# Attention and token/channel mixer on one core: a new fixed order for every engine's queue

## The chip, the cores and the metric

The kernel runs on 1 core of one Trainium2 chip. The metric is the device time of one execution in microseconds (us), as the median of the runs shown. The engines that the text speaks of are TensorE (PE, with its weight loads as PEld), VectorE (DVE), ScalarE (ACT), GpSimd (POOL) and SyncE (SP), which issues all DMAs of this kernel.

## What is computed

Attention with a decay, for 8 batches x 8 heads of 576 tokens x 64, and behind it a mixer over tokens and one over channels. All inputs are float32.

```python
def _attn_ref(q, k, v, f):                       # q, k, v: (8, 8, 576, 64), f: (8, 8, 576)
    scores = scale * np.matmul(q, k.transpose(0, 1, 3, 2))
    cum = np.cumsum(np.log(np.clip(f, 0.0001, 1.0)), axis=-1)
    decay = cum[:, :, :, None] - cum[:, :, None, :]
    scores = np.where(causal, -1000000000.0, scores + decay)
    attn = np.exp(scores - np.max(scores, axis=-1, keepdims=True))
    attn = attn / (np.sum(attn, axis=-1, keepdims=True) + 1e-09)
    return np.matmul(attn, v)

def _moe_ref(x, w_tok1, w_tok2, w_ch1, w_ch2):   # x: (8, 576, 512), the heads side by side
    xt = x.transpose(0, 2, 1)
    u = x + (np.maximum(xt @ w_tok1, 0.0) @ w_tok2).transpose(0, 2, 1)
    return u + np.maximum(u @ w_ch1, 0.0) @ w_ch2
```

The weights come as float64 and are decoded on the chip: w_tok1 is 576 x 256, w_tok2 256 x 576, w_ch1 512 x 1536, w_ch2 1536 x 512.

## The kernel before, in words

**Stages.** Head by head (n = 0 to 63) the kernel computes the scores of five query tiles (64 rows and four times 128), cut to the columns that the causal mask leaves. One PE operation makes tile 4 (`s4`), one tiles 0 and 3 (`s3`), one tiles 2 and 1 (`s2`), all at L1083. DVE takes the negated row maximum (L1085), ACT the exponential with its sum (L1088), DVE the reciprocal (L1092, L1095), POOL scales (L1110), PE transposes (L1130, L1163), ACT and DVE copy the transposes into SBUF, and PE multiplies with v (L1187, L1224). The first four heads multiply in float32 from q and k as loaded (tile `xt`, lines L1061 and L1189 to L1197 of the trace); the others split q, k and v into a high and a low part (`hl`, `vv`). After four heads half of a batch's token mixer follows (`mixer`), after eight the rest and two of the twelve column blocks of the channel mixer. Behind the last head come 512 tokens of the channel mixer in the plain way, and then four steps of 1024 tokens with a seven-product scheme (`big`), lines L1544 to L1546 and L1606 to L1608 of the trace.

**The weights** are decoded between the heads: a DMA of the raw float64 words (L817), an ACT step (L829), two DVE steps (L833, L837), and for the token mixer's weights a high part on ACT (L729) and a low part on POOL (L735).

**The order.** `build` makes a list of 5697 operations with their engine, an estimated duration, what they read and write, and the rotating buffers that they use. Each has a number from the table `PR` (kind k0 to k127, one number for each operation of the kind), which replaces the planner's due time. `Plan.run` replays the list: at each moment an engine that is free takes, among the operations that are ready and whose buffers are free, the one with the lowest number. An operation that isn't ready is passed over. The operations are then emitted in the order of the replay, under a manual schedule, so on the chip each engine runs its queue in that order and waits at each instruction for what it needs. In the table before, the numbers of each engine are all different, and they are the places in which the trace shows that engine's instructions.

**Buffers.** `run` gives each operation its buffers, the first that is free. Heads 0 and 2 share one buffer for q and k (`qf`), heads 1 and 3 the other. Scores of tiles 0 to 3, transposes and mixer products rotate through four banks of PSUM (`one`); the scores of tile 4 have one pair of banks (`sc`).

**Idle products.** `idle` (L803) is a product of 16 x 128 whose result nobody reads. `PRM["FILL"]` = 112 of them go ahead of the first real PE operation; later ones go where the replay has PE idle for more than 0.5 us (0.7 us behind 50 us), a gap's length less a margin, divided by 65 or 85 ns, up to the channel mixer.

**The first places of SP's queue**, with the size of each load, are those that the change moves most:

| place | before | KB | after | KB |
|---|---|---|---|---|
| 0, 1 | f, two halves | 72 each | f, two halves | 72 each |
| 2 | w_tok1 | 128 | w_tok1 | 128 |
| 3 | raw q, k of heads 4, 5 (half) | 288 | w_tok1 | 256 |
| 4 | w_tok1 | 128 | w_tok1 | 128 |
| 5 | w_tok1 | 256 | **q, k of head 0** | 288 |
| 6 | w_tok1 | 256 | raw q, k of heads 4, 5 (half) | 288 |
| 7 | w_tok1 | 256 | raw q, k of heads 4, 5 (half) | 288 |
| 8 | raw q, k of heads 4, 5 (half) | 288 | w_tok1 | 256 |
| 9 | **q, k of head 0** | 288 | w_tok1 | 256 |
| 10 | **q, k of head 1** | 288 | **q, k of head 1** | 288 |
| 11 | v of heads 0, 1 | 320 | w_tok1 | 256 |
| 12 | decay rows of head 4 | 4.5 | w_tok2 | 288 |
| 13 | w_tok1 | 256 | **q, k of head 2** | 288 |
| 14, 15 | w_tok2; decay rows of head 5 | 288; 4.5 | decay rows of head 2 | 2.25 each |
| 16 | gather for head 4 | 288 | v of heads 0, 1 | 320 |
| 17 to 19 | decay rows; w_tok2; gather | 4.5; 288; 288 | w_tok2; gather; q, k of head 3 | 288 each |
| 20 | **q, k of head 2** | 288 | w_tok2 | 288 |
| 21, 22 | decay rows of head 2 | 2.25 each | decay rows of head 3; gather | 2.25; 288 |
| 23 | v of heads 2, 3 | 320 | w_tok2 | 288 |

v of heads 2 and 3 stands at place 37 after, behind weight loads at places 34 and 35.

Of the kernel before, what the change touches and what calls it, by code (L numbers as in the profile page):

```python
# [15 lines left out]
P = 128  # L16

PRM = dict(
    P1=(-60, -56, -52, -48, -44), P2=(-12, -8, -4, 0, 4), E1="DDDDD", E2="DDDDD", TK=4, TU=5, PE=0, HS=(-4, -3, 19, 21), XS=(0.5, 0.6, 12, 20), HE="DDDD", XE="DDDD", WE="D", CE="D", RE="P", FILL=112, ED=False, EP=3, DB=0, DLAST=1, F1=2, FQ=4, FV=4, LAG=3.88, n_raw=1, n_vr=2, n_hl=1, n_k1=2, n_k2=2, n_vv=2,
# [5 lines left out]
    k1=(0, 1,),  # L25
# [3 lines left out]
    k5=(2,),  # L29
    k6=(3,),  # L30
    k7=(4,),
    k8=(6,),
    k9=(1, 0,),
    k10=(4, 7, 2, 6,),
    k11=(1, 3, 5, 8, 9, 10,),
    k12=(2, 4, 5, 6, 7, 13, 14, 18, 24, 31, 34, 37, 38, 39, 40, 43, 55, 57, 56, 58, 75, 73, 72, 74, 91, 108, 121, 123, 122, 124, 128, 126, 132, 127, 145, 160, 180, 178, 183, 184, 179, 181, 182, 185, 209, 215, 239, 236, 240, 232, 238, 235, 241, 233, 286, 287, 299, 296, 300, 298, 309, 311, 310, 312, 329, 338,),
    k13=(3, 5, 10, 11, 14, 17, 21, 29, 40, 43, 53, 55, 61, 72, 86, 85, 111, 178, 179, 206, 223, 254, 269, 299, 303, 347, 359, 390, 396, 470, 476, 499, 509, 543, 564,),
    k14=(8, 7, 13, 16, 21, 25, 33, 42, 52, 53, 63, 67, 81, 82, 99, 129, 142, 216, 217, 244, 250, 306, 305, 348, 346, 410, 411, 477, 478, 527, 529, 564, 566, 615, 649,),
    k15=(10, 9, 15, 19, 24, 27, 45, 44, 54, 56, 65, 71, 83, 104, 106, 143, 185, 218, 224, 246, 277, 309, 307, 364, 380, 412, 414, 511, 512, 530, 549, 582, 601, 618, 653,),
    k17=(8, 7, 12, 15, 19, 22, 39, 38, 47, 48, 58, 63, 79, 98, 104,),  # L40
    k18=(12, 11, 13, 14, 15, 16, 28, 27, 34, 35, 36, 43, 49, 59, 64,),
    k19=(11, 23, 47, 59, 67, 77, 89, 104, 114, 142, 156, 174, 195, 211, 229, 256, 271, 285, 302, 328, 343, 360, 373, 394, 410, 421, 438, 455, 465, 478, 491, 502,),
    k20=(11, 5,),
    k21=(6, 4,),
    k22=(9, 10, 20, 26,),
# [12 lines left out]
    k35=(44, 64, 82, 96,),  # L58
    k36=(22, 21, 28, 29,),
    k37=(62, 64, 68, 118, 123, 124, 184, 186, 190, 249, 251, 254, 328, 329, 332, 380, 383, 388, 466, 469, 476, 507, 513, 517, 582, 584, 590, 637, 638, 642, 704, 711, 722, 768, 771, 774, 845, 854, 857, 894, 905, 907, 968, 983, 986, 1010, 1011, 1013,),  # L60
    k38=(101, 103, 152, 157, 214, 216, 278, 279, 353, 354, 403, 405, 484, 488, 523, 531, 594, 595, 644, 645, 703, 708, 760, 763, 830, 837, 871, 883, 942, 955, 973, 974,),
    k39=(109, 112, 172, 175, 240, 242, 311, 312, 393, 394, 445, 447, 538, 542, 581, 588, 663, 664, 712, 713, 783, 788, 846, 848, 918, 925, 964, 976, 1041, 1053, 1069, 1070,),
    k40=(109, 158, 222, 281, 358, 412, 493, 534, 601, 646, 719, 766, 839, 885, 957, 976,),
    k41=(116, 176, 248, 314, 397, 455, 546, 592, 670, 717, 800, 851, 927, 978, 1054, 1072,),
# [32 lines left out]
    k74=(509, 519,),  # L97
    k75=(106, 161, 218, 288, 339,),
    k76=(195, 239, 285, 328, 377, 427, 486, 507, 558, 598,),
    k77=(243, 276, 344, 367, 446, 476, 547, 599, 650, 667,),  # L100
    k78=(144, 159, 201, 210, 258, 270, 308, 336, 361, 370,),
    k79=(130, 189, 244, 313, 362,),
    k80=(376, 380, 381, 382, 529, 530, 531, 544, 545, 547,),
# [25 lines left out]
    k106=(526,),  # L129
# [1966 lines left out]
```

## Time and profile before

| | us |
|---|---|
| median of 3 runs (lowest, highest) | 1028.75 (1024.60, 1030.69) |
| span of the profiled execution, from its first to its last instruction | 1021.2 |
| PE busy in it | 1007.6 |
| DVE, ACT, POOL busy | 813.4, 694.8, 421.4 |
| mean granted TensorE clock, as a share of the full one | 0.999 |

The page gives of the profiled execution the span, not its time with what lies around it. A busy time is the sum of an engine's instructions with overlaps counted once; PE's includes the idle products. Rows of the timeline merge instructions of one line: start, length, engine, line, operation, shapes, count, and in brackets how long the engine stood idle ahead of the first and what ended that.

### The profile page before, as it was taken

What the parts mean: (1) busy time and instruction counts of PE and PEld (TensorE: products, weight loads), DVE (VectorE), ACT (ScalarE), POOL (GpSimd) and SP (SyncE); (2) the same over time, 40 slices, a digit from 0 to 9 for tenths busy, and PEclk for the clock granted to TensorE, in tenths of its full rate; (3) what the DMA queues carried; (4) which work ended last, traced back from release to release, by engine and by line L of the source; (5) the groups of instructions that cost most, each with busy time, mean ns of one, the idle gap of its engine ahead of it and who ended that gap; (6) DMA issues with size and microseconds to landing.
All of it is one profiled execution on the core that took longest, in us unless ns stands there. A gap on an engine that the chain in (4) does not pass through costs nothing.

```text
span 1021.2 us, 19368 instructions
## 1 busy us (share of the span) xinstructions
PE 1007.6 (99%) x6228; PEld 882.6 (86%) x6228; DVE 813.4 (80%) x1932; ACT 694.8 (68%) x1708; POOL 421.4 (41%) x530
## 2 busy tenths in 40 slices
PE   8999999999999999999999999999999999999998
PEld 6588998999999999999999988888888888888886
DVE  7789889888999887987896557959669766976694
ACT  6898888888988787878896444664375546544552
POOL 6689778687787686877881100000000000000000
PEclk9999999999999999999999999999999999999999
DMA  8765788876787766554665467825832762474154
GB/s 235 253 214 200 280 307 269 292 266 253 252 280 288 254 224 235 196 192 149 218 222 200 163 225 252 288 73 195 259 103 84 231 210 83 139 250 138 31 171 139
DMA packets 110597, 212.23 MB, mean 208 GB/s; under 512 B 13296, under 2 KB 51184, under 8 KB 109472
## 3 DMA queue, kind: packets, MB, share of 16 engines
q1 hardware_dynamic: 110496, 210.99, 61.4%
q8 instruction: 50, 0.82, 0.3%
q14 instruction: 51, 0.42, 0.1%
HBM read 113.26 MB, written 44.04 MB: 154 GB/s over the span
## 4 chain that ended last, share of the span: by engine, by line
PE 82%; DVE 7%; ACT 4%; POOL 2%; DMA 2%; issue 2%; SPq 0%; DVEq 0%; POOLq 0%; ACTq 0%
PE bank L1117 8%; PE bank L1606 6%; PE bank L1607 6%; PE bank L1544 6%; PE bank L1608 6%; PE bank L1545 6%; PE bank L1546 6%; PE bank L1061 5%; PE pair L1199 2%; PE pair L1061 2%; PE pair L1201 2%; ACT pr L1075 2%; PE bank L1785 2%; PE bank L1787 2%; PE bank L1786 2%
## 5 line engine op out<-in xcount | busy, mean ns | idle before, releaser
L1103 POOL TENSOR_SCALAR pr<-pr,rec 128x192 f32<-128x192 f32 (+4 forms) x320 | 165.6, 532 | 65.4 <-DVE rec L1096 27.3
L729 ACT ACTIVATE p<-bank 128x384 fp32r<-128x384 f32 (+3 forms) x300 | 129.1, 474 | 21.6 <-PE bank L1117 18.7
L1117 PE MATMUL bank<-ident,pr 128*128 128x128 f32 (+1 forms) x960 | 139.4, 274 | 1.8 <-DVE ring L738 1.0
L1075 ACT ACTIVATE pr<-bank,nmin 128x320 f32<-128x320 f32 (+3 forms) x256 | 118.3, 470 | 14.3 <-DVE nmin L1068 13.4
L1117 PEld LDWEIGHTS bank<-ident,pr 128*128 128x128 f32 (+1 forms) x960 | 106.4, 131 | 18.4 <-ACT pr L1075 2.5
L1068 DVE CUSTOM_DVE_ANT_0 bank<-bank,mask 128x448 f32<-128x448 f32 (+3 forms) x256 | 106.3, 434 | 14.5 <-PE bank L1061 9.4
L738 DVE TENSOR_TENSOR p<-bank,p 128x384 fp32r<-128x384 f32 (+1 forms) x180 | 105.0, 590 | 10.5 <-ACT p L729 9.4
L1606 PE MATMUL bank<-ring,w2r 128*128 128x512 f32 x242 | 94.2, 389 | 0.4 <-issue 0.4
L1607 PE MATMUL bank<-ring,w2r 128*128 128x512 f32 x242 | 94.2, 389 | 0.0
L1608 PE MATMUL bank<-ring,w2r 128*128 128x512 f32 x234 | 91.2, 390 | 0.0
L1061 PE MATMUL bank<-k 128*128 128x320 f32 (+1 forms) x480 | 83.1, 302 | 0.4 <-ACT pr L1075 0.2
L1201 PE MATMUL pair<-p,vv 128*128 128x512 f32 x240 | 75.6, 322 | 0.0
L980 POOL TENSOR_TENSOR hl<-raw,hl 128x1152 fp32r<-128x1152 f32 x27 | 72.3, 2678 | 1.1
L729 ACT ACTIVATE ring<-h 128x512 fp32r<-128x512 f32 x73 | 44.5, 628 | 41.3 <-PE bank L1608 16.0
L1199 PE MATMUL pair<-p,vv 128*64 128x512 f32 x240 | 69.4, 330 | 0.0
L729 ACT ACTIVATE ring<-xt 128x512 fp32r<-128x512 f32 (+1 forms) x83 | 52.3, 648 | 23.8 <-DVE xt L1512 8.4
L1061 PEld LDWEIGHTS bank<-k 128*128 128x128 f32 (+1 forms) x480 | 62.9, 176 | 3.9 <-DVE low L738 1.0
L738 DVE TENSOR_TENSOR low<-bank,p 64x512 fp32r<-64x512 f32 (+1 forms) x120 | 52.7, 443 | 8.8 <-ACT p L729 7.0
L729 ACT ACTIVATE ring<-bank 128x288 fp32r<-128x288 f32 (+2 forms) x96 | 46.9, 498 | 17.6 <-PE bank L1787 6.9
L1075 ACT ACTIVATE pr<-pair,nmin 128x576 f32<-128x576 f32 x64 | 47.3, 739 | 15.0 <-DVE nmin L1068 12.7
L735 POOL TENSOR_TENSOR ring<-xt,ring 128x576 fp32r<-128x576 f32 x32 | 45.8, 1439 | 21.6 <-ACT ring L729 20.4
L1606 PEld LDWEIGHTS bank<-ring,w2r 128*128 128x128 f32 x242 | 45.4, 188 | 10.3 <-ACT w2r L729 0.8
(197 smaller groups left out, 3046.9 us busy)
## 6 DMA issues: line engine op xcount, KB each, us to landing
k<-hl SPq DMA_DIRECT2D x180, 288.0 KB
w2r<-sd SPq DMA_DIRECT2D x80, 256.0 KB
raw<-in_qk SPq DMA_DIRECT2D x60, 288.0 KB
w2r<-wd SPq DMA_DIRECT2D x60, 256.0 KB
vr<-in_v SPq DMA_DIRECT2D x32, 320.0 KB
ud<-xt SPq DMA_DIRECT2D x8, 1152.0 KB
pd<-part SPq DMA_DIRECT2D x32, 288.0 KB
dd<-in_w_ch SPq DMA_DIRECT2D x12, 512.0 KB
```

What stands on the lines that cost most here:

```text
L729: nc.scalar.activation(out, in_, func, scale=scale)
L738: nc.vector.tensor_tensor(out, in_, asf(hi), op=ALU.subtract)
L1061: nc.tensor.matmul(ps[:m, of : of + w], k[:, 0, i0 : i0 + m], k[:, 1, j0 : j0 + w], start=(x == 0), stop=(fq or x == 1))
L1068: nc.vector.tensor_tensor_reduce(x, x, E["mask"][:m, a : a + w], -1.0 / D**0.5, 3e38, op0=ALU.add, op1=ALU.min, accum_out=E["nmin"][sm][:m ...
L1075: nc.scalar.activation(at(pr)[:m, poff[t] : poff[t] + w], at(buf)[:m, of : of + w], AF.Exp, bias=E["nmin"][sm][:m, t : t + 1], scale=-1.0, ...
L1103: nc.gpsimd.tensor_scalar(x, x, r, 0.0, op0=ALU.mult, op1=ALU.add)
L1117: nc.tensor.transpose(out, at(pr)[:, poff[i] + start[j] : poff[i] + end[j]], E["ident"])
L1199: nc.tensor.matmul(x[:D], at(vv)[:, v0 + j, :D], at(pb)[:, 1, c0 : c0 + w], start=False, stop=last)
L1201: nc.tensor.matmul(x, at(vv)[:, v0 + j, :], at(pb)[:, 0, c0 : c0 + w], start=False, stop=last)
L1606: nc.tensor.matmul(o_, wh[:, ms], h_, start=first and pr == 0, stop=False, skip_group_check=not first)
L1607: nc.tensor.matmul(o_, wl[:, ms], h_, start=False, stop=False, skip_group_check=not first)
L1608: nc.tensor.matmul(o_, wh[:, ms], l_, start=False, stop=pr == PH - 1, skip_group_check=not first)
```

## The change

The table PR has new numbers for 115 of its 127 kinds. As before, the numbers of one engine are all different. `Plan.run` now sorts each engine's operations by number and takes them strictly in that order: an operation that isn't ready or has no buffer holds its engine's queue in the replay too. Of the buffers it takes the one that comes free first, and it places at each step the engine whose next operation can start earliest. The idle products ahead of the first PE operation follow from the replay's start of that operation.

The kinds that the text speaks of: k20 and k21 copy the decay rows of heads 0 and 1 into place on DVE (L1018) and ACT (L1017); k5 loads the table of the exponential on ACT; k22 loads q and k of heads 0 to 3 (L1038), k36 the decay rows of heads 2 and 3 (L1023), k19 v for two heads (L1003), all on SP; k13, k14 and k15 are decode steps.

```diff
-    k5=(2,),
+    k5=(5,),
...
-    k20=(11, 5,),
-    k21=(6, 4,),
-    k22=(9, 10, 20, 26,),
+    k20=(5, 16,),
+    k21=(4, 10,),
+    k22=(5, 10, 13, 19,),
...
-    k36=(22, 21, 28, 29,),
+    k36=(15, 14, 21, 24,),
...
     def run(self, slots):
...
+        queue = {e: [] for e in ("PE", "DVE", "ACT", "POOL", "SP")}
+        for o in sorted(self.ops, key=lambda o: (o.prio, o.idx)):
+            queue[o.eng].append(o)
...
-                for s in slots[b.kind]:
-                    if all(free_at(u, o.eng) <= t and u not in taken for u in s):
-                        break
-                else:
+                best = None
+                for s in slots[b.kind]:
+                    if taken.intersection(s):
+                        continue
+                    f = max(t, max(free_at(u, o.eng) for u in s))
+                    if best is None or f < best[0] - 1e-9:
+                        best = (f, s)
...
+        for _ in range(len(self.ops)):
+            best = None
+            for e, q in queue.items():
+                if head[e] == len(q) or q[head[e]].need:
                     continue
...
+                x = place(q[head[e]])
...
+                if best is None or t < best[0]:
+                    best = (t, e, x[1])
...
-                for _ in range(PRM["FILL"] if at_ == 0 else int((gap - g0) / g1) if gap > g2 else 0):
+                for _ in range(33 + int(max(0.0, o.start - 7500) / 66) if at_ == 0 else int((gap - g0) / g1) if gap > g2 else 0):
                     E["idle"](at_ == 0)
```

## Rows read from the trace of the kernel before

**Rows 1.** The page, part 1: busy us (share of the span) x instructions.

```profile
PE 1007.6 (99%) x6228; PEld 882.6 (86%) x6228; DVE 813.4 (80%) x1932; ACT 694.8 (68%) x1708; POOL 421.4 (41%) x530
```

**Rows 2.** Windows: stretch and length, busy by engine, granted clock, DMA share, GB/s.

```profile
0.00:5.80 5.80, 4.67 (x35) 4.15 (x36) 3.72 (x13) 2.62 (x4) 5.00 (x14) 1.00 0.45 129
5.80:13.00 7.20, 6.80 (x85) 5.36 (x84) 5.22 (x10) 5.47 (x11) 4.84 (x7) 1.00 0.98 264
13.00:19.50 6.50, 5.98 (x23) 3.85 (x24) 5.85 (x23) 3.73 (x12) 1.45 (x2) 1.00 0.87 277
...
22.34:60.00 37.66, 37.66 (x195) 22.75 (x195) 29.70 (x100) 32.75 (x102) 24.89 (x39) 1.00 0.76 243
60.00:560.00 500.00, 494.87 (x3796) 466.59 (x3796) 434.53 (x1250) 421.39 (x1166) 379.00 (x463) 1.00 0.68 239
560.00:1000.00 440.00, 438.99 (x1999) 364.77 (x1998) 323.92 (x518) 222.81 (x403) 4.20 (x3) 1.00 0.53 172
...
1016.90:1021.20 4.30, 0.00 (x0) 0.00 (x0) 0.37 (x1) 0.00 (x0) 0.00 (x0) 0.80 0.32 116
```

**Rows 3.** Windows of line L803 alone, the idle products: stretch, PE and PEld busy.

```profile
1.10:4.90 3.80, 3.70 (x33) 3.44 (x33) 1.00 0.55 153
7.30:12.70 5.40, 5.20 (x79) 4.71 (x79) 1.00 1.03 279
19.50:22.34 2.84, 2.02 (x28) 1.72 (x28) 1.00 0.93 298
60.00:560.00 500.00, 0.93 (x10) 0.57 (x10) 1.00 0.68 239
560.00:600.00 40.00, 1.10 (x16) 1.01 (x16) 1.00 0.43 156
```

**Rows 4.** The chain that ended last, near the start: start, us, what.

```profile
17.84 4.37 DMA xt<-cc
```

**Rows 5.** Timeline of ACT and DVE near the start.

```profile
5.34 1.28 ACT L770 ACT_TABLE_LOAD   x1
5.43 1.35 DVE L772 TENSOR_TENSOR_SCAN cc<-xt 64x576 f32<-64x576 f32 x1 [0.82 <-ACT xt L768]
10.32 0.45 DVE L1018 TENSOR_SCALAR xt<-cc 1x576 f32<-1x576 f32 x1
17.15 0.44 ACT L829 ACTIVATE dd<-dd 128x256 f32<-128x256 f32 x1 [0.69 <-DMA dd<-in_w_tok]
17.80 0.73 ACT L1075 ACTIVATE pr<-pair,nmin 128x576 f32<-128x576 f32 x1
21.32 0.15 DVE L1093 TENSOR_SCALAR rec<-sums 128x6 f32<-128x6 f32 x1
```

**Rows 6.** Timeline of SP near the start: loads of q and k.

```profile
5.64 1.23 SPq L1038 DMA_DIRECT2D xt<-in_qk  x2
16.11 0.53 SPq L1038 DMA_DIRECT2D xt<-in_qk  x1
```

**Rows 7.** Timeline of PE: the first scores.

```profile
13.00 1.25 PE L1061 MATMUL bank<-xt 97*64 97x64 f32 x4 [0.40 <-ACT dd L829]
...
15.05 3.10 PE L1061 MATMUL bank<-xt 97*128 97x320 f32 x12
```

**Rows 8.** A wait at 160 us: DVE's and PE's timeline, and line L837's durations (min/median/max).

```profile
159.60 1.84 DVE L837 SCALAR_TENSOR_TENSOR dd<-dd 128x512 uint32<-128x512 uint32 x1
162.16 0.39 PE L1716 MATMUL bank<-ring,held 128*128 128x256 f32 x1 [1.40 <-DVE ring L738]
L837 DVE SCALAR_TENSOR_TENSOR dd<-dd x35: 385/674/1891, 9.5 to 331.7; 128x512 uint32<-128x512 uint32 x22, 128x256 uint32<-128x256 uint32 x9, 128x288 uint32<-128x288 uint32 x4
```

**Rows 9.** SP: its waits (first 100 us) and weight loads; PE: head 2's product with v.

```profile
SPq L1028 <- PE pair L1190: 13.5, 3, 5.2
28.73 6.92 SPq L817 DMA_DIRECT2D dd<-in_w_ch  x4
45.24 1.07 PE L1189 MATMUL pair<-part,vr 64*64 64x512 f32 x2
```

More of the change, by code (lines that the diff above doesn't have):

```diff
@@ L24 @@
     k0=(0,),
-    k1=(0, 1,),
+    k1=(1, 0,),
     k2=(0,),
@@ L28 @@
     k4=(1,),
-    k5=(2,),
+    k5=(5,),
     k6=(3,),
-    k7=(4,),
-    k8=(6,),
+    k7=(9,),
+    k8=(11,),
     k9=(1, 0,),
[L34 to L37, printed above, removed]
@@ L583, in run, with place @@
                     fifo[k][b] = len(fifo[k])
+        tail = port_at = 0.0
+        dma_at = 1000.0
+        ends, lands = [0.0] * 3, [0.0] * 8
+        order = []
         def free_at(u, eng):
-            x = busy_unit.get(u)
-            return x[0] + self.LAT[x[1]][eng] if x else 0.0
-        def place_all(o):
-            got, taken, nx = [], set(), {}
+            x = unit.get(u)
+            if x is None:
+                return 0.0
+            return x[0] + self.LAT[x[1]][eng] if x[1] else float("inf")
+        def place(o):
+            t, got, taken, nx = max(o.ready, engine_at[o.eng]), [], set(), {}
             for b in o.bufs:
@@ new lines, in run @@
+        for _ in range(len(self.ops)):
+            best = None
+            for e, q in queue.items():
+                if head[e] == len(q) or q[head[e]].need:
+                    continue
+                x = place(q[head[e]])
+                if x is None:
+                    continue
+                t = max(x[0], port_at) if q[head[e]].port else x[0]
+                if best is None or t < best[0]:
+                    best = (t, e, x[1])
+            if best is None:
+                raise RuntimeError(f"no operation can start: {len(order)} of {len(self.ops)} placed")
+            t, e, got = best
+            o = queue[e][head[e]]
+            head[e] += 1
+            for b, s in got:
+                b.slot = s
+                k = self.GROUP.get(b.kind, b.kind)
+                if k in fifo:
+                    nexts[k] = fifo[k][b] + 1
+                for u in s:
+                    unit[u] = (0.0, None)
+            o.start = t
+            if e == "PE":
+                o.start = t + max(0.0, max(o.ready, t - tail) + o.head - t)
+                tail = o.tail
+            if e == "SP":
+                o.start = max(t, lands[-8] + 60)
+                end = max(o.start + o.dur, ends[-3])
+                dma_at = max(end + 270, dma_at) + o.lat
+                done = dma_at + 1400
+                lands.append(done)
+                if o.lat > 300:
+                    ends.append(dma_at)
+            else:
+                end = o.start + o.dur
+                done = end + o.lat
+            engine_at[e] = end
+            if o.port:
+                port_at = end
+            order.append(o)
+            for d in o.outs:
+                d.need -= 1
+                d.ready = max(d.ready, done + self.LAT[e][d.eng])
+            for b in o.bufs:
+                b.rel.append((done, e))
+                b.left -= 1
+                if b.left == 0:
+                    for u in b.slot:
+                        unit[u] = max(b.rel)
```

321 lines of the change are left out of this document (117 added, 204 removed).

## The prediction

> **What bounds the kernel now.** I read the busy times first. TensorE (PE) is busy 99% of the span [rows 1], so only what stands inside that 99% without being needed, and the missing 1%, can be won. The table by stage comes second [rows 2]. From 560 to 1000 us PE is busy 438.99 of 440 us with products of the channel mixer that the change leaves as they are: next to nothing to win there. From 60 to 560 us it is busy 494.87 of 500, with VectorE (DVE) at 434.53 and ScalarE (ACT) at 421.39: full, but the others are close behind. From 22.34 to 60 us PE is busy all the time. So a lead gained before 22 us is kept only if DVE and ACT can run ahead by as much. The third view counts the idle products (L803) as work that isn't needed [rows 3]: 33 + 79 ahead of the first score, 28 more between 19.50 and 22.34, then 10 and 16. Last the chain of waits: the piece just ahead of PE's first long run is a DMA, the decay rows of head 2 (xt<-cc) from 17.84 to 22.21 [rows 4]. The beginning, some 22 us of which PE's real work is 5.5 (two heads' scores), is the one place where PE waits long.
>
> **The change part by part.**
>
> *The rule itself costs nothing and brings nothing.* On the chip each engine takes its queue in order in both kernels. The old numbers of PR are already the places at which the trace shows the instructions: the decay rows on DVE (L1018) have places 5 (head 1) and 11 (head 0), and head 0's row runs late, at 10.32 us [rows 5]. What changes is therefore the order alone, the buffer that each operation gets, and the count of idle products. Comparing the two tables, 666 of 1375 PE operations keep their place, and the mean shift is 1.0 place on PE, 1.9 on ACT, 2.3 on DVE, 3.1 on GpSimd (POOL) and 4.5 on the DMA queue (SP): small moves everywhere, large ones at the very start.
>
> *Head 0's inputs.* Its q/k load goes from place 9 to 5 of SP's queue. It was issued behind 5.64 us [rows 6]. By the queue's sizes it was the end of 2032 KB (2081 kB) in order, and the first score that needs it ran at 13.00 [rows 7]; by then 5.8 x 129 + 7.2 x 264 = 2649 kB had moved [rows 2], since later loads share the engines: a ratio of 0.79. Now 944 KB (967 kB) stand up to its end; 967 / 0.79 = 1224 kB, reached at 5.8 + (1224 - 748) / 264 = 7.6 us. The DVE row of head 0, now behind the scan and one decode step, and the ACT row are ready by about 7.9 (the scan ends at 6.78, a row takes 0.45 on DVE and more on ACT [rows 5]). So head 0 starts near 8.0 instead of 13.00: 5.0 us. The idle products shrink with it: the formula gives 33 + (8000 - 7500) / 66, some 40 in place of 112. They are no gain of their own: in the old kernel they ended just ahead of a load that was late anyway.
>
> *Head 1.* Its load ends the same 2320 KB (2376 kB) as before: 2376 / 0.79 = 3008 kB, at 13 + 359 / 277 = 14.3 us. It began at about 15.9 (a third into the twelve products that start at 15.05 [rows 7]). This is 1.6 us earlier, and the least that the start can bring.
>
> *Head 2.* Its load waits for head 0's buffer, so it was issued at 16.11, when head 0's scores were over, with its decay rows behind it [rows 4, 6]. In front of it 1184 KB fewer stand now (a v load, two gathers, a weight load): 1212 kB at 277 GB/s are 4.4 us. Its scores start at about 17.9 in place of 22.34: the most that the start can bring, 4.5 us.
>
> *Which of the two.* Head 0's exponentials decide, because its transposes are what PE does next. In the old order ACT waits for a weight load until 17.15, runs without a gap from there, and the first reciprocal comes at 21.32 [rows 5]. In the new order that load has a v load less in front (320 KB, 328 / 277 = 1.2 us), the exponential of 576 columns (0.73) passes ahead of it, and of the decode steps between the exponentials three fewer stand there (0.44 each [rows 5]): 1.2 + 0.7 + 1.3 = 3.2 us, of which a little goes into the wait for the second weight load. I take 3.0, between 1.6 and 4.5. The reserve that has to hide the rest: PE is full from 22.34 to 60 while the 16 DMA engines are busy 76% and DVE and ACT 79% and 87% there [rows 2], so the next heads' loads can come 3 us earlier too.
>
> *The body.* Here the edit is some thousand exchanges of neighbours. What they can win is bounded by PE's time that is not work: 500 - 494.87 = 5.1 us, 440 - 438.99 = 1.0 us, and 0.93 + 1.10 us of idle products [rows 2, 3], 8.2 us in all. The lower end is below nothing, since every exchange also moves instructions that now just fit. The largest single wait shows how: at 159.60 a decode step on DVE (L837) takes 1.84 us, against a median of 0.674 for this line, and PE stands 1.40 us behind it [rows 8]. The two orders are nearly the same there (the decode steps go 6 to 10 places ahead on DVE), so such a hit may go, or turn up elsewhere. I take 3.0 us, a little over a third of the bound. With no row for the new neighbours this is an estimate between -4 and +8.2.
>
> *Moves that cost.* On SP the second v load goes from place 23 to 37, behind weight loads that wait for a raw buffer: four of them took SP from 28.73 to 35.65 [rows 9]. It is needed by the product with v of head 2, at 45.24 [rows 9], with the lead at 42. That leaves 6 us for the transfer of 320 KB, which at 243 GB/s [rows 2] is 1.4: I cost it at nothing, and a rival below at more. On ACT two decode steps and head 0's row now run ahead of the exp table's load (1.28 [rows 5]); no exponential can run before head 0's scores and their minima, near 9, so it is hidden; without that cover it would cost its 1.28.
>
> *Sum.* 3.0 + 3.0 = 6.0 us. Against the profiled execution the span goes from 1021.2 to about 1015.2. The median of the runs stands 7.5 us above that span; I let this stay as it is: 1028.75 - 6.0 = 1022.7 us.
>
> **A rule that speaks against it.** In the rows the 33 products of 1.1 to 4.9 take 112 ns each and the 79 of 7.3 to 12.7 take 66 [rows 3], about the two levels of 1.2 and 2.4 GHz, and the granted clock falls again only behind the last product, 0.80 in the last 4.3 us [rows 2]. In the new order PE has a hole from head 0's last score (8.0 + 2.9 = 10.9) to head 1's load at 14.3. Between 13 and 60 us the old trace shows the granted clock at 1.00 throughout, and its idle time of 19.50 to 22.34 was filled with 28 products. If the new hole is filled likewise (the program does it where its replay sees a gap over 0.5 us), nothing happens; if not, the clock could fall there. The Trainium skill, page "TensorE: Matmul & The Clock Gate", section "Part 1: The HAM clock gate", says that an engine left idle is put back to the lower level and that activity brings it back; by that rule, an unfilled hole would make the next products twice as long.
>
> **The rivals.**
>
> *A. The lead is given back.* DVE (434.53) and ACT (421.39 of 500 us) are the next in line [rows 2], and a wait for them takes the place of the one removed. For it: their 84 to 87%. Against it: 13 to 16% of 500 us are far more than 3 us. Only the least start (1.6 us) stays and the body brings nothing, or loses 1: 1028.
>
> *B. The body pays in full.* All 8.2 us and 4.5 at the start: 1016. For it: the waits of PE are many and short, the kind that exchanges of neighbours can remove. Against it: DVE's hits like the one at 159.60 come from instructions that meet, and no order fixes when they meet.
>
> *C. SP holds a load too long (slower).* SP's places move most (4.5 in the mean). A DMA that waits holds all that is queued behind it on SP, up to 5.2 us in the first 100 us (the decay rows behind a product with v [rows 9]). The place is head 2's product with v, and the like of it later. One hold costs up to 5.2 us once the row lands behind 42 us; from the third hold on it outweighs 6.0 + 5.1: 3 x 5.2 - 6.0 = 9.6 us more than before, 1038. For it: place 23 to 37. Against it: 60 to 560 us shows the DMA at 68%.
>
> *D. The clock falls in the hole.* Heads 1 and 2 (2.9 us each) take twice as long: 4 to 5.8 us, so about 1027. For it: the hole of 3.4 us. Against it: the program fills gaps that its replay sees.
>
> **How the numbers follow.** Forecast (1019 to 1026, likeliest 1022.7): 0.46; A (1028): 0.20; B (1016): 0.20; C (1038): 0.08; D (1027): 0.06. A measurement of this kernel can tell about 0.5%, 5.1 us, from no change: the bound for faster is 1023.6. Of the forecast's 0.46 some 0.27 lie below it; with B's 0.20 this makes 0.47 for faster. The forecast's other 0.19, A and D make 0.45 for the same, and C 0.08 for slower. For the range I leave out C and a little of B's far end: 1014 to 1031.
>
> **What would show it.** Right: first score near 8 us, head 1 near 14.3, head 2 near 18, about 40 idle products ahead of the first score, PE full from about 20 us, and a span near 1015. The start is wrong if head 2 starts behind 21 us or if PE shows holes between 20 and 60 us. The body is wrong if PE's time not busy from 60 to 560 us is not below 5.1 us; C is shown by a product with v or a score whose releaser is a DMA; D by a granted clock below 1.00 ahead of 60 us. The prediction as a whole is wrong if the lead at 60 us and the lead at 1000 us differ by more than the 4 us that the body may lose.

## The result, and the profile after

| | before | after |
|---|---|---|
| median of 4 runs (lowest, highest) | 1026.67 (1023.74, 1030.69) us | 1016.32 (1015.61, 1017.58) us |
| after / before | | 0.9898 [0.9868, 0.9929] |
| span of the profiled execution | 1021.2 us | 1014.0 us |

The change makes the kernel 10.35 us, 1.0%, faster. The direction and the range were right. The gain is over the 6.0 us forecast, and 1016 was the number of rival B.

The kernel after has 30 lines fewer ahead of these: L1061 is now L1031, L837 is L807, L803 is L773, L738 is L708, L1075 (the exponentials) is L1045, L980 is L950, L1103 is L1073, L1117 is L1087, L1201 is L1171. First the busy times of the page, as in [rows 1]:

```profile
PE 998.8 (99%) x6146; PEld 877.6 (87%) x6146; DVE 816.7 (81%) x1932; ACT 687.5 (68%) x1708; POOL 428.2 (42%) x530
```

PE has 82 products fewer, mostly the idle ones ahead of the first score, and is busy 8.8 us less. Next the windows by stage, with the columns of [rows 2]:

```profile
0.00:5.80 5.80, 4.67 (x35) 4.16 (x36) 3.73 (x13) 2.17 (x3) 4.50 (x13) 1.00 0.56 136
5.80:13.00 7.20, 6.98 (x42) 4.36 (x42) 6.29 (x18) 6.59 (x12) 4.73 (x8) 1.00 0.99 267
13.00:19.50 6.50, 5.89 (x29) 3.44 (x26) 6.40 (x20) 4.32 (x16) 3.02 (x5) 1.00 0.88 261
19.50:22.34 2.84, 2.11 (x12) 1.51 (x12) 2.59 (x11) 2.84 (x12) 2.84 (x6) 1.00 0.99 287
22.34:60.00 37.66, 37.44 (x207) 23.24 (x205) 32.06 (x102) 35.03 (x106) 26.83 (x41) 1.00 0.82 270
60.00:560.00 500.00, 492.91 (x3816) 468.32 (x3815) 436.92 (x1242) 420.91 (x1156) 383.59 (x461) 1.00 0.67 233
560.00:1000.00 440.00, 438.68 (x1974) 364.70 (x1974) 323.26 (x522) 215.69 (x408) 2.73 (x2) 1.00 0.57 178
```

Two lines matter. In 22.34 to 60 us PE stays all but full (37.44 of 37.66 us) while DMA, DVE and ACT are busier than in [rows 2] (0.82 against 0.76, 32.06 against 29.70, 35.03 against 32.75): the reserve that the prediction counted on was used. In 60 to 560 us PE is busy *less* than before (492.91 against 494.87), and yet the kernel gains there; the experiments come back to that. Now PE's timeline at the start, against [rows 7] and [rows 4]:

```profile
8.72 1.25 PE L1031 MATMUL bank<-xt 97*64 97x64 f32 x4 [0.22 <-DMA xt<-in_qk]
...
11.50 2.00 PE L773 MATMUL pair<-lower 128*16 128x128 f32 x29
13.90 1.10 PE L1031 MATMUL bank<-xt 97*128 97x320 f32 x4 [0.40 <-ACT pr L1045]
...
17.34 2.11 PE L1031 MATMUL bank<-xt 97*64 97x64 f32 x8 [0.16 <-DMA xt<-cc]
20.10 1.24 PE L1031 MATMUL pair<-xt 97*128 97x288 f32 x4 [0.64 <-ACT pr L1045]
21.17 2.10 PE L1087 MATMUL bank<-ident,pr 128*64 128x128 f32 x12
```

Head 0 starts at 8.72 (13.00 before), head 1 at 13.90, head 2 at 17.34 (22.34 before), and from 21.17 to 60 us PE stands idle for 0.35 us in all. The hole between heads 0 and 1 is filled with 29 idle products, and the granted clock is 1.00.

The tool for the rest is the **lead**: the start of each PE operation in before's trace less the start of the same operation in another trace. It says where time is gained, which no total does. In us, by the time in before's trace (for the kernels described below):

```
time before   after   after again   before again   rule only   start new   body new   112 idle   later steps
 54.9          3.85      3.57          0.23          0.23         3.90       -5.91      -0.23       4.09
105.9          3.50      3.24         -0.11         -0.02         3.32       -7.07      -0.54       5.08
122.5          1.17      3.23         -1.85         -1.80         2.00       -7.20      -1.20       3.95
186.7          3.39      5.48         -1.84         -1.77         2.02       -4.91       1.08       6.64
279.9          3.56      5.00         -3.94         -3.35         1.95       -5.03       1.36       5.59
407.5          5.98      7.42         -3.62         -3.11         2.05       -2.56       3.84       7.70
562.5          6.29      7.49         -3.66         -3.18         1.92       -3.82       0.80       8.19
1015.7         6.45      8.57         -3.18         -3.70         0.68       -2.17       2.18       8.82
```

### The profile page after: what moved, and what is told of

It reads as the page before. It is cut to its first block, busy times and chain, and to the rows that moved or that the text cites. A ratio compares the mean times of both kernels' runs of the same rounds, so it can differ in the third digit from the quotient of the medians.

```text
span 1014.0 us, 19130 instructions
## 1 busy us (share of the span) xinstructions
PE 998.8 (99%) x6146; PEld 877.6 (87%) x6146; DVE 816.7 (81%) x1932; ACT 687.5 (68%) x1708; POOL 428.2 (42%) x530
## 4 chain that ended last, share of the span: by engine, by line
PE 83%; DVE 8%; ACT 3%; issue 2%; DMA 2%; POOL 1%; SPq 0%; DVEq 0%; POOLq 0%; ACTq 0%
PE bank L1087 8%; PE bank L1576 6%; PE bank L1578 6%; PE bank L1577 6%; PE bank L1514 6%; PE bank L1516 6%; PE bank L1515 6%; PE bank L1031 5%; PE pair L1031 3%; PE pair L1169 3%; PE pair L1171 2%; ACT pr L1045 2%; PE bank L1686 2%; PE bank L1783 2%; PE bank L1687 2%
## 5 line engine op out<-in xcount | busy, mean ns | idle before, releaser
L1073 POOL TENSOR_SCALAR pr<-pr,rec 64x64 f32<-64x64 f32 (+4 forms) x320 | 171.6, 551 | 47.7 <-DVE rec L1066 18.2
L1087 PE MATMUL bank<-ident,pr 128*128 128x128 f32 (+1 forms) x960 | 140.4, 274 | 4.7 <-DVE low L708 2.6
L1045 ACT ACTIVATE pr<-bank,nmin 64x64 f32<-64x64 f32 (+3 forms) x256 | 118.3, 471 | 12.5 <-DVE nmin L1038 10.4
L1087 PEld LDWEIGHTS bank<-ident,pr 128*128 128x128 f32 (+1 forms) x960 | 106.4, 131 | 21.6 <-DVE low L708 2.9
L708 DVE TENSOR_TENSOR p<-bank,p 128x384 fp32r<-128x384 f32 (+1 forms) x180 | 105.3, 590 | 10.6 <-ACT p L699 10.1
L1038 DVE CUSTOM_DVE_ANT_0 bank<-bank,mask 128x448 f32<-128x448 f32 (+3 forms) x256 | 106.5, 432 | 6.2 <-PE bank L1031 4.8
L1578 PE MATMUL bank<-ring,w2r 128*128 128x512 f32 x244 | 94.9, 389 | 0.0
L1031 PE MATMUL bank<-k 128*128 128x320 f32 (+1 forms) x480 | 83.3, 303 | 0.7 <-ACT pr L1045 0.6
L1576 PE MATMUL bank<-ring,w2r 128*128 128x512 f32 x212 | 82.5, 389 | 0.0
L1577 PE MATMUL bank<-ring,w2r 128*128 128x512 f32 x212 | 82.5, 389 | 0.0
L699 ACT ACTIVATE ring<-xt 128x512 fp32r<-128x512 f32 (+1 forms) x86 | 54.6, 649 | 35.8 <-DVE xt L1482 18.0
L1171 PE MATMUL pair<-p,vv 128*128 128x512 f32 x240 | 76.4, 321 | 0.0
L950 POOL TENSOR_TENSOR hl<-raw,hl 128x1152 fp32r<-128x1152 f32 x27 | 72.5, 2684 | 1.4
L1031 PEld LDWEIGHTS bank<-k 128*128 128x128 f32 (+1 forms) x480 | 62.3, 176 | 3.3 <-ACT pr L1045 0.9
L699 ACT ACTIVATE ring<-h 128x512 fp32r<-128x512 f32 x63 | 38.3, 626 | 38.5 <-DVE h L1541 16.9
L708 DVE TENSOR_TENSOR low<-bank,p 64x512 fp32r<-64x512 f32 (+1 forms) x120 | 52.3, 442 | 10.8 <-ACT p L699 9.0
L702 POOL TENSOR_SCALAR p<-low 64x576 fp32r<-64x576 f32 x60 | 40.5, 676 | 40.2 <-DVE low L708 27.8
L1045 ACT ACTIVATE pr<-pair,nmin 128x576 f32<-128x576 f32 x64 | 47.3, 739 | 10.2 <-DVE nmin L1038 7.1
```

The costliest lines, as they stand in the source:

```text
L699: nc.scalar.activation(out, in_, func, scale=scale)
L708: nc.vector.tensor_tensor(out, in_, asf(hi), op=ALU.subtract)
L1031: nc.tensor.matmul(ps[:m, of : of + w], k[:, 0, i0 : i0 + m], k[:, 1, j0 : j0 + w], start=(x == 0), stop=(fq or x == 1))
L1038: nc.vector.tensor_tensor_reduce(x, x, E["mask"][:m, a : a + w], -1.0 / D**0.5, 3e38, op0=ALU.add, op1=ALU.min, accum_out=E["nmin"][sm][:m ...
L1045: nc.scalar.activation(at(pr)[:m, poff[t] : poff[t] + w], at(buf)[:m, of : of + w], AF.Exp, bias=E["nmin"][sm][:m, t : t + 1], scale=-1.0, ...
L1073: nc.gpsimd.tensor_scalar(x, x, r, 0.0, op0=ALU.mult, op1=ALU.add)
```

## The experiments

My theory after the result: the start brings a lead of about 3.9 us, which is kept; the body brings a few us more. The rest of the 10.35 us comes from the base, since before's profiled execution was one of its quick ones. The rivals: the rule brings something by itself; the new count of idle products is the start's gain; the body's gain is DVE steps that are no longer held by POOL.

**e1: the new rule with the old numbers**, and 112 idle products as in before. The edit is shown against after, with one of its 115 kinds:

```diff
-    k22=(5, 10, 13, 19,),
+    k22=(9, 10, 20, 26,),
...
-                for _ in range(33 + int(max(0.0, o.start - 7500) / 66) if at_ == 0 else int((gap - g0) / g1) if gap > g2 else 0):
+                for _ in range(112 if at_ == 0 else int((gap - g0) / g1) if gap > g2 else 0):
```

> The new replay rule with the old numbers and 112 idle products: each engine's queue is the old one, only the buffers chosen and the filled gaps differ. Theory (the order is all): the time of the kernel before within 0.3%, first score at 13.0 us, head 2 at 22.3. Rival (the rule and its choice of buffers help by themselves): 3 us or more faster than before.

Measured: 1024.2 us (1022.37 to 1029.92, 12 runs), ratio 0.9989 [0.9972, 1.0006]. The rule alone brings nothing that these runs can tell from none, and not the 3 us of its rival.

**e2: the new order for all that starts in the first 60 us, the old order behind it**; **e3: the reverse**, old start and new body. All 127 kinds are merged that way; of k15, the decode steps on DVE, the first 17 show it:

```diff
# e2, against before
-    k22=(9, 10, 20, 26,),
+    k22=(5, 10, 13, 19,),
-    k15=(10, 9, 15, 19, 24, 27, 45, 44, 54, 56, 65, 71, 83, 104, 106, 143, 185,
+    k15=(7, 8, 17, 19, 25, 24, 48, 46, 52, 58, 66, 70, 84, 102, 105, 143, 185,
# e3, against before
-    k15=(10, 9, 15, 19, 24, 27, 45, 44, 54, 56, 65, 71, 83, 104, 106, 143, 185,
+    k15=(10, 9, 15, 19, 24, 27, 45, 44, 54, 56, 65, 71, 83, 104, 106, 141, 185,
```

> New order for all that the replay starts within its first 60 us, old order behind it. Theory (the start is a gain that is kept): about 4 us less span than before, 0.4%, with PE's lead of 3.9 us at 57 us still there at 560. Rival (the lead is given back because DVE and ACT can't run ahead, and the gain is the body's): less than 1.5 us faster, the lead gone by 200 us.

> Old order for the first 60 us of the replay with 112 idle products, new order behind it. Theory (start and body add up): some 3 us less span than before and 4 us more than the changed kernel, first score at 13.0. Rival (the body alone carries the gain): as fast as the changed kernel within 0.2%.

Measured: e2 1022.24 us, ratio 0.9972 [0.9956, 0.9989]; e3 1019.76 us (1017.64 to 1024.49), 0.994 [0.9919, 0.9961]. The sum of the two gains, 0.28% and 0.60%, is a little under the 1.0% of the whole. e2 is 2.8 us below the kernel before beside it, where the theory had about 4. In e2 the lead is 3.90 at 55 us, falls to 2.00 by 122 us and stays there until 560: most of the loss, 1.3 us, comes with one DVE step that is held for 2.31 us at 115.3. The other traces with the old body lose as much there, the one of before alone doesn't (see e5); over before again and rule only, e2 leads by 3.3 us or more all along, though its median is only 2.0 us below that of rule only. In e3 the lead grows from -5.91 to -2.17, 3.7 us. Why does it begin at -5.91? Its profiled execution is the longest of the six (1024.49 us, mean clock 0.995). Its rows, of ACT, of PE and as windows:

```profile
25.77 0.46 ACT L799 ACTIVATE dd<-dd 128x288 f32<-128x288 f32 x1 [2.77 <-DMA dd<-in_w_tok]
```

```profile
27.57 1.75 PE L1087 MATMUL bank<-ident,pr 128*128 128x128 f32 x7 [1.91 <-ACT pr L1045]
```

```profile
27.00:38.00 11.00, 10.43 (x25) 4.23 (x26) 3.44 (x10) 5.19 (x19) 4.07 (x7) 0.53 0.58 194
```

A weight load landed late; the decode step that waits for it stands on ACT ahead of head 2's exponentials; PE stood idle 1.91 us; and behind that the granted clock was 0.53 in the mean of 11 us, close to the lower of its two levels (1.2 and 2.4 GHz). That is rival D's mechanism, in the *old* start. The new order has this decode step behind the first two of head 2's five exponentials. Such a fall is the likely cause of before's long executions, though none of them left a trace: of 69 beside these experiments 8 had a mean clock of 0.995 or less, and they took 1028.58 to 1033.40 us; the median of those above 0.995 is 1024.5. With the new start none of 37 was below 0.997.

**e4: after, with 112 idle products** ahead of the first score.

```diff
-                for _ in range(33 + int(max(0.0, o.start - 7500) / 66) if at_ == 0 else int((gap - g0) / g1) if gap > g2 else 0):
+                for _ in range(112 if at_ == 0 else int((gap - g0) / g1) if gap > g2 else 0):
```

> The changed kernel with 112 idle products ahead of the first score instead of 34. Theory (the products hold head 0 until 12.7 us, head 1 then starts at 15.6 instead of 13.9, and only that is lost): 1.7 us slower than the changed kernel. Rival (head 2's loads wait for head 0's scores, so all of the start's gain goes): 3.5 us or more slower. Rival (the fewer products cost clock): faster than the changed kernel.

Measured: 1020.03 us (1018.29 to 1020.58), ratio 0.9942 [0.9925, 0.996]: 3.7 us above after, 5.6 above after again (e6). My theory had 1.7 us and missed; the number is that of the rival with head 2's loads. PE's timeline:

```profile
8.00 5.20 PE L773 MATMUL pair<-lower 128*16 128x128 f32 x79
13.12 1.28 PE L1031 MATMUL bank<-xt 97*64 97x64 f32 x4
...
24.18 1.24 PE L1031 MATMUL pair<-xt 97*128 97x288 f32 x4 [0.84 <-ACT pr L1045]
```

and of SP the issue of head 2's load of q and k, in after and in e4:

```profile
11.83 0.48 SPq L1008 DMA_DIRECT2D xt<-in_qk  x1
```

```profile
16.27 0.48 SPq L1008 DMA_DIRECT2D xt<-in_qk  x1
```

The lead at 55 us is -0.23: the whole gain of the start is gone. With the old count the idle products themselves hold PE until 13.1 us, and the early load is worth nothing. Head 2's load waits for head 0's scores and goes out 4.4 us later, and the 29 idle products between heads 0 and 1, right for the new start, now keep head 1 until 17.98 us.

**e5 and e6: before and after once more**, unchanged.

> The kernel before once more, for a second trace of it. Theory (which decode step on DVE is held by a long POOL instruction differs from execution to execution): other instructions of line L837 over 1.2 us than those at 159.60 and 261.10 of the first trace, and PE's place against the first trace jumps where they stand. Rival (the hits belong to the order): the same two, within 0.3 us of their length.

> The changed kernel once more, with a second trace. Theory: 8 to 10 us faster than before, 0.8 to 1.0%; head 2's first score again near 17.3 and the lead at 57 us again near 3.9, while the decode step at 115.51 (3.84 us) is shorter by over 1 us or gone. Rival (hits belong to the order): 3.84 us again, within 0.3.

Measured: e5 1026.08 us (one execution; the median of eleven others of before beside it is 1024.93, from 1023.37 to 1033.40), span 1024.3. e6 1014.43 us (1012.42 to 1017.43), ratio 0.9894 [0.9866, 0.9922], span 1011.9. Two traces of one program differ by 3.1 and 2.1 us, and this is where. In e5, DVE and PE:

```profile
118.68 2.73 DVE L837 SCALAR_TENSOR_TENSOR dd<-dd 128x512 uint32<-128x512 uint32 x1
```

```profile
122.94 0.66 PE L1117 MATMUL bank<-ident,pr 128*128 128x128 f32 x4 [1.65 <-DVE low L738]
...
273.00 0.76 PE L1061 MATMUL bank<-k 128*128 128x320 f32 x4 [2.00 <-ACT part L1820]
```

Neither stall is in the trace that the prediction used. Both hold back e5's lead for good (-1.85, then -3.94).

But the two hits of the first trace, at 159.60 and 261.10, are in e5 as well (161.48 us, 1.82 long, and 263.00, 1.58 long): for them my theory missed, and the rival, that hits belong to the order, is right. So it is in all seven traces with the old body (before, before again, e1, e2, e8, e9, e11): the steps near 160 and near 263 us are held in each (1.80 to 1.88 and 1.56 to 1.89 us), and one near 118 us in all but that of before (2.21 to 2.97 us, with PE idle for 1.06 to 1.89 behind it). The new body has its own: where they were not moved, the step near 74 us (2.67 to 2.75) and the one near 257 us (2.96 to 3.75) are held in each of its traces. Most holds are fixed by the order, and a few differ from execution to execution.

One that differs: in after and in after again, the same instruction, DVE first and POOL second, first the trace of after:

```profile
115.51 3.84 DVE L807 SCALAR_TENSOR_TENSOR dd<-dd 128x512 uint32<-128x512 uint32 x1
...
114.62 1.55 POOL L1073 TENSOR_SCALAR pr<-pr,rec 128x448 f32<-128x448 f32 x3
116.15 2.65 POOL L950 TENSOR_TENSOR hl<-raw,hl 128x1152 fp32r<-128x1152 f32 x1
...
120.28 0.66 PE L1087 MATMUL bank<-ident,pr 128*128 128x128 f32 x4 [2.09 <-DVE low L708]
```

and that of after again:

```profile
115.76 0.70 DVE L807 SCALAR_TENSOR_TENSOR dd<-dd 128x512 uint32<-128x512 uint32 x1
...
115.23 2.04 POOL L1073 TENSOR_SCALAR pr<-pr,rec 128x448 f32<-128x448 f32 x3
```

3.84 us or 0.70 us, by how two engines happen to meet, with 2.09 us of PE behind the long one. Of the six traces that have this step in this place, two show it held (after and e10). In the second trace POOL was the one that waited: its three scalings took 2.04 us instead of 1.55.

**e7: after, with POOL's product of 1152 columns (L950 for q and k) split into two of 576.**

```diff
-    ..., lambda hl=hl, raw=raw, el=el: lo_on(el, at(hl)[:, 1::2, :], at(raw), at(hl)[:, 0::2, :]),
+    ..., lambda ...: [lo_on(el, at(hl)[:, 2 * x + 1, :], at(raw)[:, x, :], at(hl)[:, 2 * x, :]) for x in (0, 1)],
```

> The changed kernel with POOL's longest instruction (the low part of q and k, 1152 columns, 2.65 us, 27 times) as two of 576 columns. Theory (a decode step on DVE waits for the POOL instruction that runs): no step of L807 and its like over 2.5 us, the sum of DVE's excess over its medians about half of the 11 us of the first trace of the changed kernel, and 1 to 3 us faster than the changed kernel. Rival (DVE is held by something else): steps of 3 us and more as before, time as the changed kernel or a little slower for 27 more starts of 0.1 us on POOL.

Measured: 1014.69 us (1012.23 to 1018.84), ratio 0.9895 [0.9864, 0.9927]: no better than after; the theory (1 to 3 us faster, no step over 2.5 us) missed. Two holds over 2.5 us stayed. The longest, with DVE (two instructions of this line, 3.75 and 0.68) and POOL:

```profile
256.51 4.35 DVE L807 SCALAR_TENSOR_TENSOR dd<-dd 128x512 uint32<-128x512 uint32 x2
...
255.46 2.74 POOL L1073 TENSOR_SCALAR pr<-pr,rec 128x576 f32<-128x576 f32 x6
258.17 1.54 POOL L950 TENSOR_TENSOR vv<-vr,vv 128x640 fp32r<-128x640 f32 x1
```

The step began at 256.51 and ended at 260.26, half a microsecond behind the last of five POOL instructions that followed one another without a gap. Four of the five had begun after it: it is held by POOL's *row* of instructions, and not by the one that runs. Whether a shorter product shortens such a hold e7 does not show, since none of the instructions that POOL ran during its three holds (at 73.79, 256.51 and 276.36 us) is a split one, and the hold at 115.5 did not come, as it does not in after again. A half takes 1.43 us where the whole took 2.67, so the split itself costs 0.18 us each time.

**e8, e9 and e11: is it PE's pause that lets the clock fall?** In e8, with e1's numbers, the weight load of e3's decode step (k12) goes six places back on SP, behind three loads of 288 KB. In e9 the decode step (k13) goes behind head 2's exponentials besides. e11 is e8 without the idle products that the program put into the pause.

```diff
# e8, against e1
-    k12=(2, 4, 5, 6, 7, 13, 14, 18, 24, 31, 34,
+    k12=(2, 4, 5, 6, 7, 13, 14, 18, 30, 31, 34,
# e9, against e8
-    k13=(3, 5, 10, 11, 14, 17, 21, 29, 40,
+    k13=(3, 5, 10, 11, 14, 17, 21, 37, 40,
# e11, against e8
-  int((gap - g0) / g1) if gap > g2 else 0):
+  int((gap - g0) / g1) if gap > g2 and not 22000 < o.start < 32000 else 0):
```

> The order of before under the new rule, with one load moved: the raw w_tok2 block of the eighth decode step (SP's place 24) goes six places back, behind three loads of 288 KB, so that it lands about 3 us later in every execution. That decode step stands on ACT ahead of head 2's exponentials. Theory (the clock falls when PE pauses here): ACT's step waits about 4 us instead of 1.28, PE pauses over 1.5 us between 25 and 30 us, the granted clock drops to 0.5 for some 10 us as in the profiled execution of e3, and nearly every execution has a mean clock of 0.993 to 0.995: 1024.2 (e1) + about 3 of pause + 5 of slow products = 1031 to 1033. Rival (only the pause counts, the fall in e3 had another cause): mean clock 0.998 or more, 1026.5 to 1028. Second rival (the pause is hidden or given back): 1024 to 1026.

> The same late load as in e8, and the decode step that waits for it moved on ACT from place 29 to 37, behind head 2's exponentials, which is about where the new order has it. Theory (it is the place of the step on ACT, not the load, that makes PE pause): no pause over 1 us between 22 and 35 us, mean clock 0.998 or more in all executions, 1023 to 1025. Rival (the load itself, or the start's other waits, bring the fall): some executions at 0.995 or below and 1030 or more.

> The late load of e8, without the 28 + 10 idle products that the program put into the pause there (between 25.9 and 29.9 us), because its replay saw that pause; nothing else differs. In e8 ACT waited 4.16 us for the load, PE's waiting was filled, the granted clock stayed at 1.00 and ten executions took 1025.9 to 1029.4 at a clock of 0.998 to 1.000. Theory (the clock falls when PE stands idle here, and idle products hold it up): PE stands idle 2 to 3 us between 26 and 29.5 us, the granted clock shows 0.5 for 3 to 10 us behind that, most executions are at 0.993 to 0.997, and the median is 2 to 5 us above e8's, 1028.5 to 1032. Rival (the fall in e3 came from something else): clock 0.998 or more, 1025.5 to 1027.5, as e8.

Measured: e8 1026.63 us (1025.94 to 1029.38, 10 runs), clocks 0.998 to 1.000. My theory had 1031 to 1033 for it, and missed: the replay saw this pause, and the program filled it. The rows of e8:

```profile
27.25 0.46 ACT L799 ACTIVATE dd<-dd 128x288 f32<-128x288 f32 x1 [4.16 <-DMA dd<-in_w_tok]
```

```profile
25.97 1.88 PE L773 MATMUL pair<-lower 128*16 128x128 f32 x28
28.71 0.55 PE L1087 MATMUL bank<-ident,pr 128*128 128x128 f32 x3 [0.86 <-DVE part L1091]
29.02 0.83 PE L773 MATMUL pair<-lower 128*16 128x128 f32 x10
...
30.89 1.28 PE L1031 MATMUL bank<-xt 97*64 97x64 f32 x4
```

Without them, in e11:

```profile
28.18 0.55 PE L1087 MATMUL bank<-ident,pr 128*128 128x128 f32 x3 [2.26 <-DVE part L1091]
...
29.77 1.86 PE L1031 MATMUL bank<-xt 97*64 97x64 f32 x4
```

```profile
28.00:34.00 6.00, 5.82 (x17) 1.98 (x17) 2.19 (x9) 4.99 (x18) 3.02 (x6) 0.72 0.71 236
```

e11 took 1028.47 us (1024.19 to 1029.99, 10 runs), 1.8 us more than e8, at the low end of what the theory gave, with clocks of 0.995 to 0.999, nine of ten at 0.998 or less. The four products of L1031 that take 1.28 us in e8 take 1.86 here, and the granted clock is 0.72 in the mean of those 6 us (1.00 in e8). So the unfilled pause lets the clock fall, and idle products hold it up. What this costs is less clear than the two medians look: e8 and e11 ran beside different executions of before (medians 1024.36 and 1025.55 us), and both stand at 1.0022 of it ([1.0007, 1.0038] and [1.0, 1.0044]); at 54.9 us e11's trace is 0.5 us behind e8's (leads of -3.07 and -2.58). In e11 it stayed down for less time than in e3, and what decides between the two lengths is open. e9, with the step behind the exponentials, took 1024.16 us (1023.07 to 1026.01, 10 runs), clocks 0.999 to 1.000: the late load costs 2.5 us where the step stands in the old order, and nothing behind the exponentials.

**e10 and e12: after, with two held decode steps moved on DVE.** e10 moves the step at 73.6 us four places back, and the next one behind that at 115.5, which so stays where it was; e12 moves that one itself, five places forward.

```diff
# e10 (k15, its steps 15 and 19)
-    ... 105, 141, 185, 215, 225, 245,
+    ... 105, 145, 185, 215, 225, 254,
# e12 (its steps 15 and 18)
-    ... 105, 141, 185, 215, 225, 245,
+    ... 105, 145, 185, 215, 220, 245,
```

> After, with two decode steps of DVE (L807) moved behind the copies that PE's next transposes wait for: the one at 73.6 us four places back, the one at 115.5 us nine places back. In two executions of after the first was held 2.71 us by POOL's running instructions and PE stood 1.41 us behind it, the second was held 3.84 us in one (PE 2.09 us) and 0.70 in the other. Theory (a held step costs only where a copy that PE needs stands behind it): PE's stall at 77 us goes, that at 120 can't come; PE's idle time from 60 to 600 us falls from 5.6 (without the second hit) by about 1.4 to 4.2; time 1 to 2.5 us below after's 1014.4 to 1016.3, that is 1012.5 to 1014.5, a ratio to before of about 0.988. Rival (hits turn up elsewhere, the next DVE instruction is held in its place): the stall stays within 0.5 us, idle time 5.6 to 7.1, 1014.4 to 1016.3.

> After, with two decode steps of DVE (L807) moved: the one held at 73.6 us four places back, as in e10, and the one held at 115.5 us (which e10 had not caught: it moved its neighbour) five places forward, so that POOL's product of 2.65 us at 116.15 is not yet near. Theory (a held step costs only where a copy that PE needs stands behind it): no stall of PE over 1 us from 60 to 140 us; its idle time from 60 to 600 us falls to about 4.2 us from 5.6 (after again, without the second hit) and 7.1 (after, with it); 1012 to 1014.5. Rival (the next instructions are held in their place): a stall over 1 us stays near 77 or 120, 1014.4 to 1016.3.

Measured: e10 1015.83 us (1014.99 to 1017.04, 4 runs), ratio 0.9912 [0.9898, 0.9927]; not below after, a miss. In its trace the step at 78.18 takes 0.67 us and PE's stall at 77 us is gone, but the other is where it was:

```profile
116.19 3.82 DVE L807 SCALAR_TENSOR_TENSOR dd<-dd 128x512 uint32<-128x512 uint32 x1
```

```profile
120.95 0.66 PE L1087 MATMUL bank<-ident,pr 128*128 128x128 f32 x4 [2.08 <-DVE low L708]
...
122.29 0.44 PE L1783 MATMUL bank<-ring,held 128*128 128x288 f32 x1
...
125.05 0.29 PE L1783 MATMUL bank<-ring,held 128*128 128x288 f32 x1
```

Here the clock fell behind a stall in the body too: the same product takes 0.44 us and, 2.8 us later, 0.29, and the granted clock is 0.58 in the mean:

```profile
120.90:125.00 4.10, 4.05 (x20) 4.04 (x21) 3.34 (x9) 3.29 (x10) 0.84 (x2) 0.58 0.90 261
```

It had also fallen at the start, in the new order, when head 2's decay rows came late:

```profile
18.65 3.55 PE L1031 MATMUL bank<-xt 97*64 97x64 f32 x8 [1.15 <-DMA xt<-cc]
```

```profile
19.00:24.00 5.00, 5.00 (x17) 3.46 (x18) 3.20 (x15) 3.60 (x14) 4.17 (x9) 0.66 0.95 264
```

The eight products that take 2.11 us in after take 3.55 here. So rival D is not gone with the new order; it is rarer and shorter (0.997 in the mean, against 0.993 to 0.995).

e12: 1013.11 us (1010.93 to 1015.47, 6 runs), ratio 0.9867 [0.9838, 0.9895]. Both steps run unheld, at 75.88 and 112.58 us, and from 20 to 250 us there is no stall of PE over 0.8 us. But a new one stands at 262.90:

```profile
262.90 0.55 PE L1087 MATMUL bank<-ident,pr 128*128 128x128 f32 x3 [1.26 <-ACT part L1790]
```

The lead over after again is 1.8 us at 106, 0.6 at 280 and 0.25 at the end: most of the gain is given back. PE's idle time from 60 to 600 us is 5.1 us, against 5.6 in after again, not the 4.2 expected. The median is the lowest of all, 1.3 us under e6's, but the intervals overlap: that e12 beats after is not shown.

**Where the body gains.** In 60 to 560 us PE is busy 494.87 us before [rows 2], 492.91 after, and in after again:

```profile
60.00:560.00 500.00, 494.37 (x3828) 469.88 (x3827) 434.21 (x1244) 421.92 (x1158) 385.63 (x462) 1.00 0.66 233
```

In after again its idle time isn't smaller than in before's trace, and yet the lead grows by 3.3 us there. The gain lies inside the busy time. For each pair of neighbouring products by shape I took the quickest tenth of the intervals between their starts, and summed what the others take longer, in us (number):

```
60 to 560 us       longer by 50-200 ns   200-400 ns   over 400 ns
before                30.5 (353)          4.3 (14)      4.4 (6)
before again          30.3 (350)          3.8 (12)      8.7 (8)
rule only             30.5 (353)          4.0 (13)      7.7 (8)
body new              27.1 (320)          3.4 (12)      6.8 (10)
after                 27.3 (326)          3.1 (10)      6.8 (7)
after again           26.8 (319)          3.3 (11)      5.5 (7)
later steps           27.5 (324)          2.5 (9)       5.2 (7)
```

The three traces with the old body have 30.3 to 30.5 us of short delays, the four with the new one 26.8 to 27.5: about 3.3 us, in every trace. Counted the same way, start new (old body) has 30.1 and 112 idle (new body) 27.1. The profile counts them as busy, since a product's modelled end reaches over them: in after, products of L1757 and L1755 that start 0.13 us apart are shown with 0.29 to 0.30 us each. The long stalls differ as much between two traces of one kernel (4.4 and 8.7; 6.8 and 5.5) as between the kernels. The columns add up: from before again to after again 3.5 + 0.5 + 3.2 = 7.2 us, and the lead between the two grows by 7.24 us from 60 to 562 us; from before to after 3.2 + 1.2 - 2.4 = 2.0, and the lead grows by 1.9. What a single short delay waits for the rows do not say; that stays open.

## Why the prediction was right, and where it was wrong

- **The start (3.0 us, between 1.6 and 4.5): right, a little low.** The lead at 55 us is 3.85, 3.57 and 4.09 with the whole new order and 3.90 in e2. The steps held within 0.8 us: head 0 at 8.72 (8.0), head 1 at 13.90 (14.3), head 2 at 17.34 (17.9); 34 idle products ahead of the first score (40). Heads 0 and 2 waited last for what was forecast, a load and the decay rows. Head 1 did not: its 14.3 was the end of its load, but PE waited for an exponential on ACT (0.40 us; in after again for its decay row on DVE, 0.48 us), so that number is right partly by luck. That PE could hide the rest was right: from 21.17 to 60 us it is idle for 0.35 us. The path that was to set it held too: the first reciprocal, reckoned 3.2 us earlier, came 3.30 us earlier than in [rows 5] (21.32):

```profile
18.02 0.15 DVE L1063 TENSOR_SCALAR rec<-sums 128x6 f32<-128x6 f32 x1
```

- **The idle products (no gain of their own): right for the old order, too short for the new.** e4 loses all of the start's lead. The prediction treated their count as a follower of the load; it is a condition.
- **The rule (nothing): right**, e1.
- **The body (3.0 us, between -4 and 8.2): the size was off for a typical execution, and the bound was read from the wrong place.** Against before's profiled execution it is 2.6 us in after, 5.0 in after again; against before again 6.0 and 8.4. The step that failed is "bounded by PE's time that is not work": PE's idle time of 5.1 us doesn't hold the 3.3 us won from short delays, and another execution of the same kernel is idle for 4.0 us more in that stretch (busy 490.89 us in before again). For the same reason the sign that I gave, idle time below 5.1 us, was a wrong one: it is 7.1 and 5.6. Wrong too was what I held against rival B, that no order fixes where the hits fall: the one at 159.60, with its PE stall of 1.40 us, is in all seven traces with the old body and in none with the new.
- **The base ("7.5 us above that span; I let this stay"): wrong.** In every execution with both numbers the time is 1.8 us above the span (1015.77 and 1014.0; 1026.08 and 1024.3). The other 5.7 us were scatter: the profiled execution had escaped two stalls of 1.65 and 2.00 us that before again has (the first of them, or its like, is in all six other traces with the old body), and the median of three lay among long executions. Two of those three took 1028.75 and 1030.69, as long as those in which a later run of before shows the fallen clock; their own clocks aren't known. Over the runs beside the experiments before stands at 1024.5 without the falls and after at 1015.7 (10 executions): 8.8 us, of which 3.7 are the start's by the leads, and the other 5.1 are put down to the body. The remaining 1.6 us of the 10.35 are put down to before's long executions.
- **Rival A** (the lead is given back) fell: 3.85 at 55 us, 6.45 at the end. **Rival B** has the number but not the way: PE's idle time didn't go. **Rival C** fell: behind 60 us no wait of PE on a DMA shows, and the longest ahead of it is 0.2 us in after. **Rival D** was taken for the new order's risk and put at 0.06; its mechanism is real, but it showed mostly in the old order, and its removal is likely part of the gain.

## What to carry to other kernels

Take a kernel's base from many executions and read its profiled one as one draw: here one trace more would have shown a span longer by 3.1 us, half of the gain forecast, and which holds belong to the order. Where an engine is 99% busy, measure the intervals between its instructions before bounding what an order can win, since the busy time hides the short delays. And put nothing that waits for a load ahead of the work that feeds the bound engine: the same late load cost 2.5 us (e8) in one place and nothing (e9) in another.

## What the runs showed of the hardware

- A DVE step of 0.68 us with two inputs in SBUF (L807) took up to 3.84 us while POOL ran instructions of 0.31 to 2.67 us back to back, and ended 0.55 us behind the last of them, also where four of the five had begun after it (e7's hold of 3.75 us). Where DVE came first, it took 0.70 us and POOL waited (after again). The Trainium skill, page "SBUF — State Buffer", section "Who interferes with whom", says that such an instruction contends with a GpSimd instruction that reads SBUF, that the contention is an exclusive lock, and that the order of issue decides who blocks. The traces agree on the contention and, in after again, on the order; they differ where the step waits for a whole row of POOL's instructions, most of which began after it.
- The granted clock fell behind pauses of PE of 1.15 us (e10, 0.66 over 5 us), 1.91 us (e3, 0.53 over 11 us), 2.08 us (e10, 0.58 over 4.1 us) and 2.26 us (e11, 0.72 over 6 us). It stayed at 1.00 behind one of 2.09 us in after, at the same place as the 2.08 (from 120.2 to 125 us), behind one of 2.00 us in before again (from 273 to 278 us), and where idle products filled the pause (e8). The Trainium skill, page "TensorE: Matmul & The Clock Gate", section "Part 1: The HAM clock gate", says that idleness puts the clock back to its lower level. The traces agree, and show that a pause of one length at one place does it in one execution and not in another.
